# The down product of a gated MLP as seven-product blocks with a transposed output

## The chip, the core and the metric

The kernel runs on one core of a Trainium2 chip. Its engines are TensorE (PE, matrix products; PEld is its weight load), VectorE (DVE), ScalarE (ACT), GpSimd (POOL) and SyncE (SP), which mostly starts transfers. The metric is the device time of a run in microseconds; the kernel before takes 717.9 us (median of 3 runs, 716.68 to 718.46).

## The reference

Rotary attention over 4 x 8 heads of 576 positions of 64, then a gated MLP over the 2304 tokens:

```python
x = attention(rotate(q), rotate(k), v)          # 2304 x 512
g = x @ w_gate                                  # 512 x 1536
silu = g * (1.0 / (1.0 + np.exp(-g)))
val = x @ w_val
out = (silu * val) @ w_out                      # 1536 x 512
```

## The kernel before

Every matrix product of the MLP is made in three passes of a 32-bit reduced format: an operand is split into a high half (a copy that rounds) and a low half (operand minus high), and hi x hi, hi x lo and lo x hi are accumulated in PSUM. The split is written `split` (line 678): the copy on ScalarE, the subtract on VectorE or GpSimd.

Attention fills the first 280 us. Then `plain` multiplies the first 256 columns of w_gate and w_val directly, while the weights of the rest are prepared. From some 336 us, `strassen` makes the other 1280 columns in ten weight steps s: pair fp = 1 + s // 2, and i = s % 2 says gate (0) or value (1). A weight step has three units, one for each third p of the tokens in the order 1, 2, 0 (`ORDER`); a third is two blocks of 384 tokens. A unit is one 2 x 2 block product in seven products (`PROD`) of six matmuls of 384 columns (line 824), each product in a PSUM bank of its own, of a ring of six. VectorE, ScalarE and GpSimd put the seven together (lines 808, 827). One unit later `finish` (line 846) applies silu where i is 0, and `keep` stores gate or value to two DRAM buffers, hf for the first 7 tiles of 128 tokens, ht for the other 11.

Beside it runs a stream of jobs (`Stream`), each one raw 512 KB block of weights: a load, a ScalarE instruction and six VectorE instructions that turn stored bits into numbers (lines 734 to 741). 20 jobs are w_gate and w_val, 12 are w_out; `strassen` takes two or three of them in a weight step.

The down product follows in `finish` (line 1341), in two stages. In the first, for each of 12 blocks f of 128 hidden rows: HF is loaded from hf (line 876), VectorE multiplies gate by value (line 882), the product and a w_out block are split, lows on GpSimd, and seven PSUM banks accumulate 3 matmuls of 512 columns each (line 892). In the second, each of 11 token tiles is loaded from ht, multiplied and split on VectorE (line 928) and gets 36 matmuls of 512 columns (line 941). Results are token rows; ScalarE copies them out of PSUM (line 901) and SP stores them.

From the last part of attention to the end, the order of instructions is the written one on all of PE, ACT, DVE, SP and POOL (`manual_schedule`); elsewhere a planner orders them by program order and the readiness that it expects. SP's queue is in written order, and a transfer at its head waits there until its buffer is free.

Of the kernel before, what the change touches and what calls it, by code (L numbers as in the profile page):

```python
# [19 lines left out]
NT = B * S  # L20
# [477 lines left out]
FT, NX = 7, 3  # L498
PROD = [(0, "B", 0), (5, "T", 3), (4, "T", 0), (6, "T", 1), (2, "T", 2), (1, "B", 1), (7, "B", 2)]


class Moe:
    def __init__(self, tc, keep, pl, yd, rd, hd, wg, wv, wo, out):
        self.tc, self.nc = tc, tc.nc
        self.yd, self.rd, self.hd, self.w, self.wo, self.out = yd, rd, hd, (wg, wv), wo, out
# [25 lines left out]
    def xbuf(self, pool, blk):  # L531
        p, b = divmod(blk, 2)
        if b == 0:
            self.xa[p] = [self.own(pool, f"xa{p}{x}", [128, 4, BK]) for x in "hl"]
        else:
            self.xm[p] = [self.own(pool, f"xm{p}{x}", [128, 2, BK]) for x in "hl"]
            self.xb[p] = [self.own(pool, f"xb{p}{x}", [128, 2, BK]) for x in "hl"]

    def wform(self, pool, i):
        self.W[i] = [self.own(pool, f"W{i}{x}", [128, 8, 256]) for x in "hl"]  # L540
# [20 lines left out]
    def open_late(self, ctx):  # L561
# [7 lines left out]
        self.WF = [self.own(one, f"WF{i}", [128, 8, 256], FP32) for i in range(2)]  # L569
# [6 lines left out]
    def open_mid(self, ctx):  # L576
# [4 lines left out]
        self.own(one, "HF1", [128, FT, 2, 128], FP32)  # L581
# [198 lines left out]
    def ev(self, u, ps):  # L780
# [9 lines left out]
        sv = sv.rearrange("p (t i q) -> p t i q", i=2, q=128)  # L790
        nc.scalar.activation(out=sv[:, :, 0], in_=ps[0].rearrange("p (t q) -> p t q", q=128), func=ACTF.Silu)
        nc.scalar.copy(sv[:, :, 1], ps[1].rearrange("p (t q) -> p t q", q=128))
        self.keep(f, 9 * s + 3 * t, sv.rearrange("p t i q -> p t (i q)"), slice(0, 2), nc.sync if u else nc.scalar)

    def keep(self, f, t, x, i, q):
        n = x.shape[1]
        m = min(max(FT - t, 0), n)
        if m:
            q.dma_start(out=self.hd[0][f, :, t:t + m, i].rearrange("p t i q -> p t (i q)"), in_=x[:, 0:m])
        if m < n:  # L800
            t = t + m - FT
            q.dma_start(out=self.hd[1][t:t + n - m, :, f, i].rearrange("t p i q -> p t (i q)"), in_=x[:, m:n])

    def unit(self, fp, i, p):
# [3 lines left out]
        add = lambda e, out, in0, in1: e.tensor_tensor(out=out, in0=in0, in1=in1, op=ALU.add)  # L808
        sg = [self.again(f"xm{p}{x}", [128, 2, BK], FP32, "sg") for x in "hl"]
        dst = [sg[k // 2][:, k % 2] for k in range(4)]  # L810
        (ah, al), (bh, bl), (Th, Tl) = self.xa[p], self.xb[p], self.T[p]
        B = [(ah[:, 0:2], al[:, 0:2]), (ah[:, 2:4], al[:, 2:4]), (bh, bl)]
        c1, u, z5 = (self.c_p.tile([128, BK], FP32, name=n) for n in ("c1", "u", "z5"))
        for k, (w, kind, x) in enumerate(PROD):
            acc = self.ch()[:, 0:BK]
# [5 lines left out]
            for c in range(2):  # L821
                rh, rl = xh[:, c], xl[c] if isinstance(xl, list) else xl[:, c]
                for l, r in ((Wh, rh), (Wh, rl), (Wl, rh)):
                    nc.tensor.matmul(acc, l[:, w, c * 128:(c + 1) * 128], r, start=(n == 0), stop=(n == 5))  # L824
                    n += 1
            if k in (0, 2):
                ac.copy((c1, None, z5)[k], acc)  # L827
            if k == 2 and self.after:
                self.after.pop(0)()
# [15 lines left out]
    def finish(self, fp, i, p, sg):
        for j in range(2):
            if i == 0:
                self.nc.scalar.activation(out=sg[j], in_=sg[j], func=ACTF.Silu)
            self.keep(2 * fp + j, 6 * p, sg[j].rearrange("p j (t q) -> p (j t) q", q=128), slice(i, i + 1), self.nc.sync)

    def osplit(self, f):
        g, k = divmod(f, 4)
        if k == 0:
            self.Ot = [self.again(f"{('W0', 'T1', 'T2')[g]}{x}", [128, 4, DM], F32R, f"O{x}") for x in "hl"]
        Oh, Ol = self.O[f] = [t[:, k] for t in self.Ot]
        return self.split(self.nc.gpsimd, Oh, Ol, self.of(f))
# [534 lines left out]
```

## Time and profile before

| | |
|---|---|
| Median of the runs | 717.9 us |
| The profiled execution | span 715.3 us |
| Busy: PE, DVE, POOL, ACT | 694.9, 539.7, 476.8, 409.1 us |
| Ten weight steps | 336.4 to 558.6 us |
| First down stage (L892) | 558.6 to 619.5 us |
| Second down stage (L941) | 619.5 to 711.3 us |

Busy times are sums over an engine's instructions. A group of instructions is named by line, engine, operation and tile (out<-in), with partitions x elements. The chain of waits is followed back from the last instruction: what stands in it was waited for. A wait names the engine that waits, its line, and what released it.

### The profile page before, as it was taken

What the parts mean: (1) busy time and instruction counts of PE and PEld (TensorE: products, weight loads), DVE (VectorE), ACT (ScalarE), POOL (GpSimd) and SP (SyncE); (2) the same over time, 40 slices, a digit from 0 to 9 for tenths busy, and PEclk for the clock granted to TensorE, in tenths of its full rate; (3) what the DMA queues carried; (4) which work ended last, traced back from release to release, by engine and by line L of the source; (5) the groups of instructions that cost most, each with busy time, mean ns of one, the idle gap of its engine ahead of it and who ended that gap; (6) DMA issues with size and microseconds to landing.
All of it is one profiled execution on the core that took longest, in us unless ns stands there. A gap on an engine that the chain in (4) does not pass through costs nothing.

```text
span 715.3 us, 12744 instructions
## 1 busy us (share of the span) xinstructions
PE 694.9 (97%) x4342; PEld 654.6 (92%) x4342; DVE 539.7 (75%) x884; ACT 409.1 (57%) x892; POOL 476.8 (67%) x473
## 2 busy tenths in 40 slices
PE   8999999999999999999799999999999999999997
PEld 7899999999999999988799999999999877888887
DVE  5888898888888887848898868778677893455451
ACT  5899998888888887357443524334243332433331
POOL 8899799999999966659976576655675767200000
PEclk9999999999999999999999999999999999999999
DMA  6887899779887895973465565646648865786671
GB/s 189 208 224 203 218 226 258 197 200 259 226 215 195 203 264 169 222 227 111 125 188 165 167 182 155 192 148 182 180 118 277 282 227 178 307 282 220 206 221 30
DMA packets 111329, 143.86 MB, mean 201 GB/s; under 512 B 17808, under 2 KB 86048, under 8 KB 111264
## 3 DMA queue, kind: packets, MB, share of 16 engines
q1 hardware_dynamic: 110240, 141.97, 69.9%
q10 hardware_dynamic: 1024, 1.07, 0.5%
q8 instruction: 35, 0.57, 0.3%
q14 instruction: 30, 0.25, 0.1%
HBM read 76.35 MB, written 42.54 MB: 166 GB/s over the span
## 4 chain that ended last, share of the span: by engine, by line
PE 77%; DVE 9%; ACT 6%; DMA 4%; POOL 1%; issue 1%; SPq 0%; DVEq 0%; ACTq 0%; POOLq 0%
PE ch L824 28%; PE ch L941 13%; PE pv L459 11%; PE sc L343 10%; PE tr L419 8%; DMA HF<-hf 3%; PE ch L892 2%; PE tr L283 2%; ACT E L376 1%; ACT N L302 1%; DVE HF L882 1%; PE ch L776 1%; POOL fl L678 1%; DVE raw L738 1%; DVE T2l L678 1%
## 5 line engine op out<-in xcount | busy, mean ns | idle before, releaser
L358 DVE TENSOR_REDUCE nmt<-sc 128x1 f32<-128x576 f32 x144 | 108.3, 752 | 20.2 <-PE sc L343 18.7
L376 ACT ACTIVATE E<-sc,nmt 128x576 f32<-128x576 f32 x128 | 97.5, 762 | 1.2 <-DVE nmt L358 1.1
L808 POOL TENSOR_TENSOR u<-u,z 128x384 f32<-128x384 f32 x30 | 30.5, 1015 | 71.3 <-DVE sg L808 69.2
L419 PE MATMUL tr<-ident,E 128*128 128x128 f32 x512 | 77.0, 273 | 0.4 <-DVE ET1l L421 0.2
L419 PEld LDWEIGHTS tr<-ident,E 128*128 128x128 f32 x512 | 61.1, 141 | 3.3 <-PE tr L283 1.4
L827 ACT COPY c<-ch 128x384 f32<-128x384 f32 x30 | 14.4, 481 | 81.6 <-PE ch L824 47.5
L200 POOL TENSOR_TENSOR t<-X,tab 128x256 f32<-128x256 f32 (+2 forms) x94 | 54.1, 597 | 10.2 <-DMA X<-in_qk_dram 6.4
L343 PE MATMUL sc<-QK 128*128 128x288 f32 x240 | 58.6, 325 | 1.3 <-ACT E L376 0.4
L420 ACT CAST ET2h<-tr 128x512 fp32r<-128x512 f32 x80 | 47.2, 590 | 15.9 <-PE tr L419 15.6
L421 DVE TENSOR_TENSOR ET2l<-tr,ET2h 128x512 fp32r<-128x512 f32 x80 | 53.2, 683 | 2.2 <-ACT ET2h L420 2.0
L678 DVE TENSOR_TENSOR hl<-hg,hh 128x384 fp32r<-128x384 f32 x44 | 25.8, 587 | 37.7 <-ACT hh L678 37.7
L941 PE MATMUL ch<-Oh,hh 128*128 128x512 f32 (+1 forms) x144 | 54.0, 375 | 0.0
L941 PE MATMUL ch<-Ol,hh 128*128 128x512 f32 (+1 forms) x144 | 53.8, 374 | 0.0
L941 PE MATMUL ch<-Oh,hl 128*128 128x512 f32 (+1 forms) x144 | 53.8, 374 | 0.0
L343 PE MATMUL sc<-N,QZ 128*128 128x288 f32 x240 | 51.4, 296 | 0.0
L202 POOL TENSOR_TENSOR rot<-rot,t 128x512 f32<-128x512 f32 (+2 forms) x47 | 47.0, 1000 | 3.7
L421 DVE TENSOR_TENSOR ET1l<-tr,ET1h 128x512 fp32r<-128x512 f32 x64 | 43.1, 686 | 6.9 <-ACT ET1h L420 6.4
L201 POOL TENSOR_TENSOR rot<-X,tab 128x512 f32<-128x512 f32 (+2 forms) x47 | 47.1, 1002 | 0.0
L678 ACT CAST hh<-hg 128x384 fp32r<-128x384 f32 x44 | 22.6, 514 | 41.5 <-DVE hg L928 41.5
L808 DVE TENSOR_TENSOR sg<-ch,u 128x384 f32<-128x384 f32 x60 | 33.4, 556 | 16.5 <-PE ch L824 13.0
L420 ACT CAST ET1h<-tr 128x512 fp32r<-128x512 f32 x64 | 36.9, 597 | 13.0 <-PE tr L419 13.0
L459 PE MATMUL pv<-ET2h,VS 128*128 128x320 f32 x128 | 40.7, 328 | 1.0 <-ACT ET2h L420 0.9
(413 smaller groups left out, 2414.7 us busy)
## 6 DMA issues: line engine op xcount, KB each, us to landing
QK<-N SPq DMA_DIRECT2D x64, 288.0 KB, 4.2
hg<-ht SPq DMA_DIRECT2D x22, 768.0 KB, 7.1
HF<-hf SPq DMA_DIRECT2D x12, 896.0 KB, 5.1
X<-in_qk_dram SPq DMA_DIRECT2D x15, 576.0 KB, 5.0
yd<-Y SPq DMA_DIRECT2D x31, 256.0 KB, 4.6
ht<-sg SPq DMA_DIRECT2D x20, 384.0 KB, 3.6
hf<-sg SPq DMA_DIRECT2D x20, 384.0 KB, 3.7
ht<-sg SPq DMA_DIRECT2D x20, 320.0 KB, 3.1
```

The lines of the kernel that those rows point to most:

```text
L200: e.tensor_tensor(out=sel(t2, u), in0=sel(x, w), in1=tb(Sn, u), op=ALU.mult)
L343: nc.tensor.matmul(ps[:, g, 0:288], l, rr[:, o + g * 288:o + (g + 1) * 288], start=(x == 0), stop=(x == len(terms) - 1))
L358: nc.vector.tensor_reduce(out=nmcol, in_=ps[:, :, 0:288], axis=AX.XY, op=ALU.max, negate=True)
L376: nc.scalar.activation(out=E.rearrange("p (a b) -> p a b", a=2), in_=ps[:, :, 0:288], func=ACTF.Exp, bias=nmcol, scale=1.0, accum_out=self ...
L419: nc.tensor.transpose(ps[:, c], E[:, o + c * 128:o + (c + 1) * 128], self.ident)
L420: nc.scalar.copy(dst[0], src)
L421: nc.vector.tensor_tensor(out=dst[1], in0=src, in1=r32(dst[0]), op=ALU.subtract)
L459: nc.tensor.matmul(st["ps"][:, 0:w], VS[:, sl, :], t, start=(x == 0), stop=(x == last))
L678: return [lambda: self.nc.scalar.copy(h, f), lambda: le.tensor_tensor(out=l, in0=f, in1=r32(h), op=ALU.subtract)]
L808: add = lambda e, out, in0, in1: e.tensor_tensor(out=out, in0=in0, in1=in1, op=ALU.add)
L824: nc.tensor.matmul(acc, l[:, w, c * 128:(c + 1) * 128], r, start=(n == 0), stop=(n == 5))
L941: self.nc.tensor.matmul(ps, l[:, f], r[:, z], start=(n == 0), stop=(n == 3 * NFF - 1))
```

## The change

The down product is made in the same seven-product scheme. A round n is a third of the tokens; in each of its seven steps k, TensorE takes a 2 x 2 block form of w_out (weights, in 128 x 128 pieces) and a form of the gated product (384 moving columns), 36 matmuls in two halves j. The result comes out transposed, hidden rows first, and the host reorders it.

- In the up product, the order of the seven products is changed, and the last three accumulate in PSUM onto banks of earlier ones (`ONTO`). The value unit multiplies by the gate at once; gate and value stay on chip, and only their product is stored, once a pair and third, for the first pair gate and value as before.
- w_out's forms are made in the job stream (`obits`: four GpSimd sums for the second half of a block), stored to DRAM from ACT's queue and loaded again in `Down.oload`.
- `strassen` takes 2 to 4 jobs in a weight step (`TAKE`), 29 in all, and none in the last.
- `Down` loads blocks B11, B21, B12, B22 of the product for each round, makes the sums and the splits of the next step during a step (`form`, `osplit`), and starts in the last weight step (`lead`). For round 0 the last piece of each block comes from the chip (`late`).
- From `strassen` on, only SP and PE keep the written order.

```diff
...
-FT, NX = 7, 3
-PROD = [(0, "B", 0), (5, "T", 3), (4, "T", 0), (6, "T", 1), (2, "T", 2), (1, "B", 1), (7, "B", 2)]
+NFP = NFF // 2
+PROD = [(0, "B", 0), (5, "T", 3), (4, "T", 0), (6, "T", 1), (1, "B", 1), (7, "B", 2), (2, "T", 2)]
+ONTO = {4: 0, 5: 2, 6: 3}
...
     def unit(self, fp, i, p):
         nc = self.nc
         ve, po, ac = nc.vector, nc.gpsimd, nc.scalar
...
+        tt = lambda e, out, in0, in1, op=ALU.add: e.tensor_tensor(out=out, in0=in0, in1=in1, op=op)
+        if i == 0:
+            g = self.G[p] = self.again(f"xm{p}", [128, 4, BK], FP32, "sg")
+            dst = [g[:, k] for k in range(4)]
+        else:
+            if self.V is None:
+                self.V = self.r_p.tile([128, 4, BK], FP32, name="R")
+            g, v = self.G[p], self.V
+            dst = [g[:, 0]] + [v[:, k] for k in range(1, 4)]
...
+        accs = []
         for k, (w, kind, x) in enumerate(PROD):
-            acc = self.ch()[:, 0:BK]
+            accs.append(accs[ONTO[k]] if k in ONTO else self.ch()[:, 0:BK])
+            acc = accs[k]
...
+            if k == 0:
+                ac.copy(u, acc)
+            elif k == 1:
+                tt(ve, u, acc, u)
+                if self.after:
+                    self.after.pop(0)()
+            elif k == 2:
+                ac.copy(z5, acc)
             elif k == 3:
+                tt(ve, dst[3], acc, u)
+                tt(po, dst[3], dst[3], z5)
+                if i:
+                    tt(po, g[:, 3], v[:, 3], g[:, 3], ALU.mult)
+            elif k == 4 and i == 0:
+                ac.activation(out=dst[0], in_=acc, func=ACTF.Silu)
             elif k == 4:
+                tt(ve, dst[0], acc, dst[0], ALU.mult)
             elif k == 5:
+                tt(ve, dst[1], acc, u)
+            else:
+                tt(ve, dst[2], acc, u)
+                self.after.append(lambda: self.finish(fp, i, p, g, v if i else None))
             yield k
 
...
+    def finish(self, fp, i, p, g, v):
+        nc = self.nc
+        if i == 0:
+            nc.scalar.activation(out=g[:, 1:4], in_=g[:, 1:4], func=ACTF.Silu)
+            return
+        nc.gpsimd.tensor_tensor(out=g[:, 1:3], in0=v[:, 1:3], in1=g[:, 1:3], op=ALU.mult)
+        if (fp, p) != (NFP - 1, ORDER[0]):
+            (nc.sync if fp < NFP - 1 else nc.scalar).dma_start(out=self.hd[p][fp - 1], in_=g)
...
+
+    def obits(self, half, fp):
+        nc, F = self.nc, self.FO
+        tt = nc.gpsimd.tensor_tensor
...
+
+        def end():
+            last()
+            if half == 0:
+                nc.scalar.dma_start(out=self.od[0][fp], in_=F[:, 0:2])
+                return
+            nc.scalar.dma_start(out=self.od[1][fp], in_=F[:, 3])
+            for o, a, b, op in ((4, 2, 3, ALU.add), (6, 0, 2, ALU.subtract), (5, 4, 0, ALU.subtract),
+                                (7, 1, 5, ALU.subtract)):
+                tt(out=F[:, o], in0=F[:, a], in1=F[:, b], op=op)
+            nc.scalar.dma_start(out=self.od[2][fp], in_=F[:, 4:8])
+        return ops + [end]
...
-    strassen(moe, J, S, Z)
-    finish(moe, S)
+    strassen(moe, J, S, Z).run()
...
+    o = [(h, fp) for fp in range(NFP) for h in range(2)]
     for s in range(10):
-        for h in range(2):
-            job("w", s, h)
-        if s in (4, 6, 8):
-            job("o", 2 + s // 2)
-    for f in (0, 1, 2, 3, 7, 8, 9, 10, 11):
-        job("o", f)
+        job("w", s, 0)
+        if s >= 4:
+            job("o", *o.pop(0))
+        job("w", s, 1)
+        if s in (5, 8):
+            job("o", *o.pop(0))
+    for x in o:
+        job("o", *x)
...
+TAKE = (2, 3, 3, 4, 3, 3, 4, 3, 4)
...
+    dn = Down(moe)
+    for q, k, f in dn.lead():
+        at(9, q, k, f)
...
-        dq = S.take(n, s < 9)
+        dq = S.take(TAKE[s], s < 8) if s < 9 else []
...
+SUMS = {2: ("TT", "B12", "B11"), 3: ("TT", "B22", "TT"), 4: ("B12", "B22", "B12"), 6: ("TT", "B21", "TT")}
+FORM = ("B11", "B21", "TT", "TT", "B12", "B22", "TT")
+OFORM = ((0, 0), (0, 1), (2, 0), (2, 1), (2, 2), (2, 3), (1, 0))
+LOAD = {2: ("B11",), 5: ("B21", "B12"), 6: ("B22",)}
+MULT = {4: ("B11",), 6: ("B21", "B12")}
+RAW = {"B11": ("T1h", 0), "B21": ("T1l", 2), "B12": ("T2h", 1), "B22": ("T2l", 3)}
+
+
+class Down:
+
+    def lead(self):
+        ve = self.nc.vector
+        return [
+            (0, 0, self.first), (0, 1, lambda: self.oload(0, slice(0, 5))), (0, 5, lambda: self.osplit(0, ve, slice(0, 5))),
+            (1, 0, lambda: self.vload(0, "xb1")), (1, 0, lambda: self.load(0, "B11")),
+            (1, 0, lambda: self.load(0, "B21")), (1, 4, lambda: self.late("B11")), (1, 4, lambda: self.late("B21")),
+            (1, 4, lambda: self.oload(0, slice(5, 6))), (1, 4, lambda: self.oload(1)),
+            (2, 0, lambda: self.load(0, "B12")), (2, 0, lambda: self.load(0, "B22")), (2, 0, lambda: self.late("B12")),
+            (2, 0, lambda: self.late("B22")), (2, 0, lambda: self.mult(0, "B11", ve)),
+            (2, 1, lambda: self.osplit(0, ve, slice(5, 6))),
+            (2, 1, lambda: self.form(0, ve)), (2, 4, lambda: self.mult(0, "B21", ve)), (2, 5, lambda: self.osplit(1, ve)),
+        ]
...
+    def oload(self, k, z=slice(0, NFP)):
...
+        h, x = OFORM[k]
+        self.nc.sync.dma_start(out=r32(self.O[k][1])[:, z], in_=self.moe.od[h][z, :, x].rearrange("f p d -> p f d"))
+
+    def osplit(self, k, e, z=slice(0, NFP)):
+        Oh, Ol = (x[:, z] for x in self.O[k])
+        self.nc.scalar.copy(Oh, r32(Ol))
+        e.tensor_tensor(out=Ol, in0=r32(Ol), in1=r32(Oh), op=ALU.subtract)
+
+    def vload(self, n, slot=None):
+        m, p = self.moe, ORDER[n]
+        for x in range(2):
...
+            self.nc.sync.dma_start(out=v, in_=m.hv[p][:, 2 * x:2 * x + 2, 1])
+            self.V[x] = v
+
+    def load(self, n, b):
+        m, p = self.moe, ORDER[n]
+        slot, k = RAW[b]
+        r = self.raw[b] = m.again(slot, [128, NFP, BK], FP32, "d" + b)
+        self.nc.sync.dma_start(out=r[:, 0], in_=m.hv[p][:, k, 0])
+        f = NFP - 2 if n == 0 else NFP - 1
+        self.nc.sync.dma_start(out=r[:, 1:1 + f], in_=m.hd[p][0:f, :, k].rearrange("f p q -> p f q"))
+
+    def late(self, b):
+        self.nc.sync.dma_start(out=self.raw[b][:, NFP - 1], in_=self.moe.G[ORDER[0]][:, RAW[b][1]])
+
+    def mult(self, n, b, e):
+        r, k = self.raw[b][:, 0], RAW[b][1]
+        e.tensor_tensor(out=r, in0=r, in1=self.V[k // 2][:, k % 2], op=ALU.mult)
+
+    def form(self, s, e, se=None):
+        k = s % 7
+        if k in SUMS:
+            o, a, b = SUMS[k]
+            se.tensor_tensor(out=self.raw[o], in0=self.raw[a], in1=self.raw[b], op=ALU.subtract)
+        src = self.raw[FORM[k]]
+        hi, lo = self.H[s % 2]
+        for z in (slice(0, 3), slice(3, NFP)):
+            self.nc.scalar.copy(hi[:, z], src[:, z])
+            e.tensor_tensor(out=lo[:, z], in0=src[:, z], in1=r32(hi)[:, z], op=ALU.subtract)
...
+    def run(self):
+        nc, m = self.nc, self.moe
+        ve, po, ac = nc.vector, nc.gpsimd, nc.scalar
+        self.open()
+        self.oload(2)
+        self.oload(3)
+        self.oload(4)
+        self.mult(0, "B12", ve)
+        self.mult(0, "B22", ve)
+        for s in range(N):
+            n, k = divmod(s, 7)
+            if n and k == 0:
+                self.mult(n, "B22", po)
+            if s + 1 < N:
+                n1, k1 = divmod(s + 1, 7)
+                if n == 0 and 0 < k < 6:
+                    self.osplit(k + 1, po)
+                self.form(s + 1, ve, ve if n1 == 0 or k1 == 3 else po)
+            if n == 0 and k < 2:
+                self.oload(k + 5)
+            if n < 2 and k == 2:
+                self.vload(n + 1)
+            for b in LOAD.get(k, ()) if n < 2 else ():
+                self.load(n + 1, b)
+            for b in MULT.get(k, ()) if n < 2 else ():
+                self.mult(n + 1, b, po)
+            for j in range(2):
...
+                if k == 0:
+                    ac.copy(t["u"], ps)
+                elif k == 1:
+                    ac.copy(t["o11"], ps)
+                    self.out(n, "o11", j)
+                elif k == 2:
+                    ac.copy(t["z"], ps)
+                elif k == 3:
+                    add(ve, t["u"], ps, t["u"])
+                elif k == 4:
+                    add(ve, t["o22"], ps, t["u"])
+                    add(po, t["o22"], t["o22"], t["z"])
+                    self.out(n, "o22", j)
+                elif k == 5:
+                    add(ve, t["o12"], ps, t["u"])
+                    self.out(n, "o12", j)
+                else:
+                    add(ve, t["o21"], ps, t["u"])
+                    self.out(n, "o21", j)
```

## Rows read from the trace of the kernel before

**Rows 1.** The page, part 1: busy us, share of the span, instructions.
```profile
span 715.3 us, 12744 instructions
...
PE 694.9 (97%) x4342; PEld 654.6 (92%) x4342; DVE 539.7 (75%) x884; ACT 409.1 (57%) x892; POOL 476.8 (67%) x473
```
**Rows 2.** The chain that ended last, in order of time: start, length, what.
```profile
355.71 200.98 PE ch L824 x1157
...
619.58 91.75 PE ch L941 x432
...
711.36 0.37 ACT o L901
```
**Rows 3.** Stages: length, busy us (instructions) of each engine, TensorE's clock, DMA share, GB/s.
```profile
core 0: us, PE busy (x) PEld busy (x) DVE busy (x) ACT busy (x) POOL busy (x), PEclk, DMA share, GB/s
300.00:320.00 20.00, 19.72 (x113) 19.08 (x111) 10.75 (x19) 8.64 (x19) 13.33 (x13) 1.00 0.91 249
336.40:358.00 21.60, 17.91 (x100) 17.01 (x100) 19.80 (x27) 10.49 (x17) 21.21 (x16) 1.00 0.41 121
...
490.00:512.00 22.00, 22.00 (x129) 22.00 (x128) 15.66 (x29) 8.94 (x15) 13.55 (x12) 1.00 0.65 191
535.00:558.40 23.40, 23.40 (x137) 23.40 (x136) 17.75 (x31) 7.23 (x14) 13.03 (x11) 1.00 0.91 284
```
**Rows 4.** TensorE's waits from 558.4 to 619.4 us: total, times, longest.
```profile
PE ch L892 <- POOL fl L678: 2.4, 4, 1.0
```
**Rows 5.** Timeline from 602 to 608 us: start, length, instruction, [idle before <-releaser].
```profile
603.29 2.11 POOL L678 TENSOR_TENSOR fl<-HF,fh 128x896 fp32r<-128x896 f32 x1 [2.84 <-ACT fh L678]
...
603.97 2.38 DVE L882 TENSOR_TENSOR HF<-HF 128x896 f32<-128x896 f32 x1 [1.78 <-DMA HF<-hf]
...
605.37 2.14 POOL L678 TENSOR_TENSOR Ol<-OF,Oh 128x512 fp32r<-128x512 f32 x1
...
605.46 0.50 PE L892 MATMUL ch<-Oh,fl 128*128 128x512 f32 x1 [0.56 <-POOL fl L678]
```
**Rows 6.** GpSimd's groups after 384 us: busy us, mean ns, idle before.
```profile
L678 POOL TENSOR_TENSOR fl<-HF,fh 128x896 fp32r<-128x896 f32 x12 | 25.5, 2125 | 17.0 <-ACT fh L678 17.0
...
L678 POOL TENSOR_TENSOR Ol<-R,Oh 128x512 fp32r<-128x512 f32 x3 | 3.9, 1299 | 0.0
```
**Rows 7.** Timeline from 327 to 362 us: GpSimd, VectorE, then ScalarE.
```profile
333.13 7.43 POOL L684 TENSOR_TENSOR R<-R 128x768 f32<-128x768 f32 x3
340.52 1.85 POOL L684 TENSOR_TENSOR Z<-xa0h,xa0l 128x768 f32<-128x768 f32 x1
342.32 1.02 POOL L684 TENSOR_TENSOR Z<-xm0h,xm0l 128x384 f32<-128x384 f32 x1
...
333.79 5.89 DVE L678 TENSOR_TENSOR T2l<-T0h,T2h 128x1536 fp32r<-128x1536 f32 x2
...
353.90 1.76 DVE L678 TENSOR_TENSOR T0l<-R,T0h 128x1536 fp32r<-128x1536 f32 x1
...
352.40 1.47 ACT L678 CAST T0h<-R 128x1536 fp32r<-128x1536 f32 x1
```
**Rows 8.** Timeline from 414 to 419 us, GpSimd and VectorE.
```profile
415.69 2.42 POOL L678 TENSOR_TENSOR W0l<-WF,W0h 128x1024 fp32r<-128x1024 f32 x1
...
417.25 0.56 DVE L808 TENSOR_TENSOR sg<-ch,u 128x384 f32<-128x384 f32 x1 [0.86 <-PE ch L824]
```
**Rows 9.** Line 892: min/median/max ns, first and last start.
```profile
L892 PE MATMUL ch<-Oh,fh x84: 389/389/402, 558.6 to 618.7; 128*128 128x512 f32 x84
```
**Rows 10.** Tile HF: min/median/max ns, first and last start.
```profile
L882 DVE TENSOR_TENSOR HF<-HF x12: 1091/1152/2382, 549.9 to 610.0; 128x896 f32<-128x896 f32 x12
```
**Rows 11.** DMA issues: queue, count, KB each, median us to landing.
```profile
HF<-hf SPq DMA_DIRECT2D x12, 896.0 KB, 5.1
...
out_dram<-o SPq DMA_DIRECT2D x2, 128.0 KB, 3.2
out_dram<-o SPq DMA_DIRECT2D x4, 64.0 KB, 2.2
```
**Rows 12.** VectorE's groups from 384 to 556.8 us: busy us, mean ns, idle before.
```profile
L808 DVE TENSOR_TENSOR sg<-ch,u 128x384 f32<-128x384 f32 x48 | 26.8, 557 | 14.9 <-PE ch L824 13.0 <-POOL WF L961 0.3
...
L737 DVE TENSOR_SCALAR aux<-aux 128x512 uint32<-128x512 uint32 x19 | 13.1, 692 | 0.2
```

More of the change, by code (lines that the diff above doesn't have):

```diff
@@ L568, in open_late @@
         self.wform(one, 0)
-        self.WF = [self.own(one, f"WF{i}", [128, 8, 256], FP32) for i in range(2)]
+        w = self.own(one, "WF", [128, 2, 8, 256], FP32)
+        self.WF = [w[:, x] for x in range(2)]
         self.Z = [self.own(one, f"T0l{c}", [128, 4, BK], FP32) for c in range(2)]
@@ L580, in open_mid @@
         self.wform(one, 1)
-        self.own(one, "HF1", [128, FT, 2, 128], FP32)
+        self.FO = self.own(one, "FO", [128, 8, 256], FP32)
         self.c_p = pool("m_cp", 2)
@@ L823, in unit @@
                 for l, r in ((Wh, rh), (Wh, rl), (Wl, rh)):
-                    nc.tensor.matmul(acc, l[:, w, c * 128:(c + 1) * 128], r, start=(n == 0), stop=(n == 5))
+                    nc.tensor.matmul(acc, l[:, w, c * 128:(c + 1) * 128], r, start=(n == 0 and k not in ONTO),
+                                     stop=(n == 5), skip_group_check=True)
                     n += 1
[L826 to L829, printed above, removed]
@@ L843, in unit @@
             yield k
[L845 to L856, printed above, removed]
@@ L884, in fdown @@
-    def fdown(self, f):
-        hh, hl = self.fs.pop(f)
-        Oh, Ol = self.O[f]
-        for t in range(FT):
-            if f == 0:
-                self.ps[t] = self.ch()
-            sl = slice(128 * t, 128 * t + 128)
-            for n, (l, r) in enumerate(((hh, Oh), (hh, Ol), (hl, Oh))):
-                self.nc.tensor.matmul(self.ps[t], l[:, sl], r, start=(f == 0 and n == 0), stop=(f == NFF - 1 and n == 2))
-            if f == NFF - 1:
-                self.give(t, slice(0, DM), self.ps[t])
@@ L896, in give @@
-    def give(self, t, z, ps):
-        nc = self.nc
-        if z.start == 0:
-            self.ot = self.again(f"xm{t % 2}{'hl'[t // 2 % 2]}", [128, DM], FP32, "o")
-        o = self.ot
-        nc.scalar.copy(o[:, z], ps)
-        s, k = divmod(t, 9)
-        if k < 8:
-            b, i = divmod(k, 4)
-            r0 = (2 * s + b) * S
-            nc.sync.dma_start(out=self.out[r0:r0 + 512, z].rearrange("(p r) d -> p r d", r=4)[:, i], in_=o[:, z])
-        else:
-            for g in range(2):
-                r0 = (2 * s + g) * S + 512
-                nc.sync.dma_start(out=self.out[r0:r0 + 64, z], in_=o[64 * g:64 * g + 64, z])
@@ L1332, in strassen @@
                 g += 1
-                t = g if s else min(g, 7) + max(0, g - 14)
+                t = min(g, 7) + max(0, g - 14) if s == 0 else g
                 run(dq, t * m // (21 if s else 14) - (m - len(dq)))
-    run(moe.after)
-    assert not own
-    for f in range(2, 4):
-        run(moe.osplit(f))
-def finish(moe, S):
-    for f in range(NFF):
-        if S.begun < len(S.jobs):
-            S.sign()
-        if f + 2 < NFF:
-            run(moe.fsplit(f + 2))
-        else:
-            moe.hload(FT + f - NFF + 2)
-        if f + 1 == NFF:
-            run(moe.hsplit(FT))
-        if f + 3 < NFF:
-            moe.fload(f + 3)
-        if S.ops:
-            run(S.take(1, False))
-        if f + 4 < NFF:
-            run(moe.osplit(f + 4))
-        moe.fdown(f)
-    for t in range(FT, 18):
-        if t + 2 < 18:
-            moe.hload(t + 2)
-        if t + 1 < 18:
-            run(moe.hsplit(t + 1))
-        moe.down(t, 1 + (t == 17))
+    while moe.after:
+        moe.after.pop(0)()
```

195 lines of the change are left out of this document (95 added, 100 removed).

## The prediction, before the run

> **What bounds the kernel now.** I read the busy table first: TensorE is busy for 694.9 of 715.3 us, the next engine for three quarters of them [rows 1]. Then the chain of waits, in order of time: from 355.71 us it is one block of 1157 matmuls of 384 columns, and at the end one of the down product's, 91.75 us without a break [rows 2]. So from 356 us on, whatever takes matmul columns away is worth its full time, unless operands come late. A matmul of 384 columns costs 200.98 / 1157 = 0.1737 us there; the granted clock is 1.00, the 2.4 GHz level, in every stretch read [rows 2, 3]. The only operands that come late in the old down product are low halves that GpSimd makes: TensorE waited 2.4 us for them, in four waits [rows 4].
>
> What stands behind that wait is the place to look at longest. At 603.29 GpSimd subtracts for 2.11 us, both operands in SBUF. VectorE starts a multiply of two SBUF operands at 603.97 and needs 2.38 us; it ends 0.95 us after GpSimd does. GpSimd's next subtract, 1.30 us elsewhere, takes 2.14, and the matmul at 605.46 comes late [rows 5, 6]. Earlier the same: two VectorE subtracts of 1536 take 5.89 us, where one takes 1.76, and the three GpSimd subtracts beside them 7.43, where alone they take 1.85 + 1.02 + 1.02 = 3.89. As 3.89 + 2 x 1.76 = 7.41, they ran strictly in turn [rows 7]. A VectorE add with one operand in PSUM is not touched: 0.56 us inside a GpSimd subtract that keeps its 2.42 us [rows 8]. I call it the shared turn.
>
> The Trainium skill, SBUF — State Buffer, section Who interferes with whom, has this as a rule: a VectorE instruction with two SBUF inputs and a GpSimd instruction that reads SBUF exclude each other, and the one that starts second is blocked until the first has ended. By that rule the two engines' times of such work are added, which speaks against this change; the sum below goes by the rows, which agree.
>
> **What the change does, priced.** *Matmuls.* The old down product runs from 558.6 [rows 9] to 619.58 + 91.75 = 711.33 [rows 2]: 152.7 us. The new one has 3 rounds x 7 steps x 2 halves x 6 blocks x 3 products = 756 matmuls of 384 columns: 756 x 0.1737 = 131.3 us, 6.25 us a step. Gain: 21.4 us if TensorE never waits. The up product keeps its 1260 matmuls, 42 a unit (7.3 us).
>
> The Trainium skill, TensorE: Matmul & The Clock Gate, section Back-to-back issue gap, gives N/2.4 + 2.5 ns for a warm stream. By it such a matmul takes 162.5 ns and the new product 122.9 us, 8.4 less; the rows have 173.7 in just this kind of stream, so I use the rows.
>
> *Operands of the down product.* All its sums, high copies and low subtracts go from SBUF to SBUF. VectorE takes 1.09 us for 896 elements [rows 10] and 1.76 for 1536 [rows 7], 1.05 ns an element: 0.56 for 384, 1.36 for 1152, 2.56 for 2304. GpSimd takes 1.30 for 512 and 2.13 for 896 [rows 6], 2.15 ns: 3.5 for 1536, 5.15 for 2304. The form of a step is two low subtracts, 2.72.
>
> Round 0. What must pass the shared turn between the moment when the last weight step frees its first unit's buffers (two units, 14.6 us, before the down product) and the start of step 6 (6 x 6.25 = 37.5 us into it), 52.1 us in all: seven forms 19.0; four sums on VectorE 10.2; five splits of w_out on GpSimd 17.5; the splits of blocks 0 and 1 on VectorE 3.7; four multiplies 2.2; GpSimd's three multiplies of 768 that finish the last units 5.5, and four short ones 4.1; two adds and a multiply in step 4, 3.0. That is 65.2 us, so step 6 comes at least 13.1 us late even if the turn is never idle. It is idle at the start: from the same moment to the w_out block of step 2 (O2), the queues must move the values of the first units 0.4 MB, two blocks 2.0, their last pieces 0.4, w_out 0.9, two more blocks 2.0 and pieces 0.4, one or two stores of 0.8 and O2 itself 0.8: 7.6 to 8.4 MB. They moved 249 GB/s at a busy share of 0.91 and 284 at 0.91, so 274 to 312 at most [rows 3]: 24 to 31 us, and some 2 us to land (64 KB take 2.2) [rows 11]. O2 is there 12 to 18 us into the down product; with 1.47 for its copy [rows 7] and 3.5 for its split, step 2, due at 12.5, starts 4 to 10 us late. From the copy on, 34 us of turn work remain (five splits, four forms, a sum, step 4's three), so step 6 starts 47 to 53 us in, 10 to 16 late: the same answer. With lows that may be written only after the step that frees their buffer, I take 16 for round 0; bounds 4 (the turn binds nothing, only the transfers) and 22.
>
> Round 1: seven forms 19.0, three GpSimd sums 15.5, a VectorE sum 2.6, four multiplies 4.1, two adds 2.0: 43.2 of 43.8 us. Round 2 up to its step 6: six forms 16.3, the same sums 18.1, a multiply and two adds 3.1: 37.5 of 37.5. In the old stretch from 558.6 to 619.6 the turn held 12 x 2.13 + 10 x 1.30 + 12 x 1.09 = 52 of 61 us [rows 6, 10], and TensorE lost 2.4 (4%) [rows 4]. At 99% it loses more: a VectorE instruction can stand 5.15 us behind one GpSimd sum, and behind it in VectorE's queue stand the adds that empty PSUM. Bounds 0 and 16 over 81 us; I take 8.
>
> *Up product.* Products 1, 7 and 2 accumulate onto banks that were read before. That saves VectorE an add a unit where i is 0, and GpSimd one of two adds. It adds a wait: the fifth to seventh product wait until ACT or VectorE has read the bank, filled two or three products (2.1 us or more) earlier; behind such a matmul stands all of TensorE's queue. The add is 0.56 us and one instruction of the weight stream before it 0.69 [rows 12], 1.25 together, so hidden by 0.8 us; 0.5 to 1 us a unit if VectorE lags. It may: weight steps 1 to 8 take 27 jobs of the stream, not 20, of six VectorE instructions of 0.69, + 29.0 us against 12 x 0.56 = 6.7 saved. VectorE was busy for 15.7 of 22 us [rows 3]; + 22.3 over 8 steps of 21.9 us makes 84%. The finishing multiplies go to GpSimd: 13.6 of 22 becomes some 19 where i is 1 [rows 3]. Eighteen stores of w_out's forms and two of the product stand in ACT's queue and wait there for GpSimd; behind them stand the copies of u and z, for which TensorE's fifth and sixth product wait. The order on the three engines is no longer the written one, which can gain or lose. Bounds -2 (of the 3.7 us lost at 336 to 358 [rows 3] half is won back) and +8; I take +2: VectorE fills, but does not overflow.
>
> *At nothing:* the stores of gate and value that become 14 of the product, the loads of hf and ht that become 12 blocks, and w_out's eight reloads: all on queues under matmuls; where that cover goes, at the start, they are in O2's lateness above. The transposed output costs no instruction here. *Tail:* the last add is 0.56 [rows 12], the copy was 0.37 [rows 2]; 192 KB leave in place of 128 (128 KB take 3.2 us, 896 KB 5.1) [rows 11]: + 0.3 in all.
>
> **Sum.** 715.3 - 21.4 + 16 + 8 + 2 + 0.3 = 720.2 us of span. The median of the runs, 717.9, lies 2.6 above this execution's span: 722.8, say 723.
>
> **Rivals.**
> *The shared turn hides.* If splits and sums fall into gaps and work done ahead covers rounds 1 and 2, only the transfers at the start cost: 715.3 - 21.4 + 7 + 0 to 4 + 1.3 + 2.6 = 705 to 709. For it: 16 of the 21 steps need no w_out split, and adds from PSUM run beside GpSimd freely [rows 8]. Against: round 0 is over-full by count, not by order. It decides if less than 52 us of round 0's work excludes each other. This is the case on the faster side.
> *The start runs dry.* Blocks come in pieces of 1 and 1.5 KB over one in-order queue, in which last pieces wait for GpSimd and two blocks for the second unit; and an engine whose order puts the multiply of an unlanded block first stalls with it. With O2 at 18 us, round 0 at + 22 and the later rounds at + 12: 733. For it: 300 to 320 us, where pieces of 1.5 KB are loaded, is the stretch with 274 GB/s for a full share [rows 3]. Against: 896 KB land in 5.1 us [rows 11].
> *VectorE overflows in the up product.* If its share passes some 95%, the short reach of the bank reuse costs 0.3 us in each of 24 units, + 7 in place of 2: 728.
> That no columns are saved is excluded by count: 648 x 512 against 756 x 384.
>
> **How the numbers follow.** Forecast (719 to 728) 0.45; turn hidden (700 to 716) 0.27; start dry (729 to 738) 0.18; VectorE overflows 0.10. A difference under 0.3% (715.7 to 720.1) is what a measurement here cannot tell from none. Faster: nearly all of the second case, 0.25. Same: the rest of it, the low edge of the forecast, and the last case where rounds 1 and 2 cost little, 0.12. Slower: what is left, 0.63. The range 706 to 736 leaves out the best of the second case and the worst of the third; the forecast's own is 719 to 728.
>
> **What would show it.** Right: the down product's block of the chain broken in round 0, TensorE released by VectorE and GpSimd at steps 2 to 6; GpSimd's splits of 1536 at 3.5 us alone and 5 to 6 beside VectorE; steps of 8 to 10 us in round 0 and nearer 6.25 later; O2 landing 12 us or more after the first down matmul. Wrong: 756 matmuls in under 140 us, or VectorE's subtracts of 1152 at 1.36 us with GpSimd busy beside them. More than 203 us from 356 us to the first down matmul would move the cause to the up product.

## The result, and the profile after

The changed kernel takes 725.9 us (median; 725.75 to 728.06) beside 717.3 for the kernel before on the same chip (716.26 to 718.46): ratio 1.013, 95% interval 1.0108 to 1.0151. Slower by 1.3%, though the down product streams an eighth fewer columns through TensorE (756 x 384 in place of 648 x 512).

The profiled execution has a span of 724.0 us, 8.7 more than before. I cut it at the first matmul of the up product, at the first of the down product, there at every 36th matmul (one step), and at the end of the last one, all from the timeline.

| Stretch, us | before | after | difference | forecast |
|---|---|---|---|---|
| start to first up matmul | 335.5 | 336.4 | + 0.9 | 0 |
| up product | 223.1 | 227.3 | + 4.2 | + 2 |
| down product | 152.7 | 156.8 | + 4.1 | + 2.6 (- 21.4 + 16 + 8) |
| tail | 4.0 | 3.5 | - 0.5 | + 0.3 |

The matmuls of one round of the new down product were counted at 43.8 us. Its three rounds took 57.8, 50.5 and 48.5: 14.0, 6.7 and 4.7 over the count.

The page, as in [rows 1]: TensorE is less busy in a longer span, and VectorE goes from 75% to 82%.

```profile
span 724.0 us, 12703 instructions
...
PE 687.5 (95%) x4414; PEld 668.3 (92%) x4414; DVE 593.7 (82%) x848; ACT 426.0 (59%) x873; POOL 541.0 (75%) x498
```

TensorE's waits in the down product (563 to 721 us: total, times, longest), where [rows 4] had 2.4 us in all:

```profile
PE ch L1437 <- DVE dWF L1378: 9.2, 4, 3.3
...
PE ch L1437 <- DVE dW L1378: 2.6, 3, 1.0
...
PE ch L1437 <- ACT du L1442: 2.0, 1, 2.0
```

So TensorE waits mostly for low halves of the product's forms (line 1378), which VectorE makes. With two short waits of 0.9 and 0.5 all waits come to 15.2 us. Of the rest of the 25.4 us over the count, some 7 are matmuls that no wait holds up and that stand 0.32 us apart in place of 0.174 (3.0, 2.2 and 1.9 us in the three rounds): TensorE's clock was at half behind the longer waits, as the last section says. Why the lows are late is in the timeline of round 0, steps 1 to 3 (GpSimd, then VectorE, then TensorE's waits):

```profile
576.70 3.46 POOL L1345 TENSOR_TENSOR dO<-dO 128x1536 fp32r<-128x1536 f32 x1 [8.74 <-ACT dO L1344]
...
580.55 4.15 POOL L1345 TENSOR_TENSOR dO<-dO 128x1536 fp32r<-128x1536 f32 x1 [0.39 <-ACT dO L1344]
...
584.66 4.57 POOL L1345 TENSOR_TENSOR dO<-dO,dW 128x1536 fp32r<-128x1536 f32 x1
```
```profile
577.72 8.21 DVE L1378 TENSOR_TENSOR dWF<-dT,dW 128x1152 fp32r<-128x1152 f32 x2 [1.34 <-ACT dW L1377]
585.96 5.70 DVE L1373 TENSOR_TENSOR dT<-dB,dT 128x2304 f32<-128x2304 f32 x1
592.92 2.63 DVE L1378 TENSOR_TENSOR dW<-dT,dH 128x1152 fp32r<-128x1152 f32 x2 [1.27 <-ACT dH L1377]
```
```profile
581.43 0.45 PE L1437 MATMUL ch<-dWF,dO 128*128 128x384 f32 x1 [3.25 <-DVE dWF L1378]
585.97 0.69 PE L1437 MATMUL ch<-dWF,dO 128*128 128x384 f32 x1 [2.38 <-DVE dWF L1378]
```

The two lows that take 2.63 us at 592.92, with GpSimd idle, took 8.21 beside two of GpSimd's splits; the sum took 5.70 where it takes 2.55 alone. It is a strict alternation, as in [rows 7]: the first split ends at 580.16, the first low 1.3 later (TensorE starts on it at 581.43); the second split 3.3 after that, at 584.70; the second low 1.2 later (585.97); the third split at 589.23, the sum at 591.66. The chain's last break, in round 2, is the same: a GpSimd sum, then a low of 1152 that takes 6.18 us in place of 1.35, behind GpSimd's next sum, and then TensorE (GpSimd's next sum, then the chain):

```profile
681.01 5.13 POOL L1373 TENSOR_TENSOR dB<-dB,dB 128x2304 f32<-128x2304 f32 x1
```
```profile
673.68 6.30 POOL dT L1373
...
680.00 1.17 ACT dW L1377
...
681.19 6.18 DVE dWF L1378
...
687.41 33.09 PE ch L1437 x179
...
720.52 0.56 DVE do L1440
```

The longest break of round 1 has another last step. GpSimd's sum takes 5.93 us, ScalarE's cast waits 6.25 us for it, u's copy stands behind that cast, and TensorE, whose second product goes on in u's bank, waits 2.04 for the copy (GpSimd, ScalarE, TensorE):

```profile
625.64 5.93 POOL L1373 TENSOR_TENSOR dT<-dB,dB 128x2304 f32<-128x2304 f32 x1 [2.04 <-DMA out_dram<-do]
```
```profile
631.60 1.15 ACT L1377 CAST dH<-dT 128x1152 fp32r<-128x1152 f32 x1 [6.25 <-POOL dT L1373]
632.66 0.47 ACT L1442 COPY du<-ch 128x384 f32<-128x384 f32 x1
```
```profile
633.19 0.44 PE L1437 MATMUL ch<-dW,dO 128*128 128x384 f32 x1 [2.04 <-ACT du L1442]
```

The low behind GpSimd's next sum then costs 0.65 more, at 638.98. So here most of the wait comes from a long sum on GpSimd (5.11 us for 2304 at 632.60, where VectorE takes 2.56) by way of ScalarE, and not from a low that stands behind it.

The stages, columns as in [rows 3] (the last two are new stretches, of rounds 0 and 2):

```profile
336.40:358.00 21.60, 17.98 (x92) 17.02 (x91) 19.03 (x25) 12.03 (x19) 21.13 (x15) 0.92 0.27 85
490.00:512.00 22.00, 21.26 (x123) 20.95 (x122) 20.15 (x36) 9.27 (x14) 15.08 (x14) 1.00 0.41 136
535.00:558.40 23.40, 23.40 (x137) 23.40 (x136) 17.25 (x28) 8.30 (x12) 10.98 (x10) 1.00 0.54 182
582.00:595.00 13.00, 9.14 (x39) 8.05 (x38) 11.69 (x4) 3.97 (x6) 7.23 (x2) 0.74 0.52 182
686.00:699.00 13.00, 11.59 (x57) 11.59 (x58) 11.34 (x7) 5.51 (x7) 3.70 (x2) 0.87 0.04 15
```

In the up product 336 to 358 has 8 matmuls fewer than before (1.4 us), and 490 to 512, full before, 6 fewer (1.0); VectorE was busy for 20.2 of those 22 us, before for 15.7.

### The profile page after: what moved, and what is told of

It reads as the page before. It is cut to its first block, busy times and chain, and to the rows that moved or that the text cites. A ratio compares the mean times of both kernels' runs of the same rounds, so it can differ in the third digit from the quotient of the medians.

```text
span 724.0 us, 12703 instructions
## 1 busy us (share of the span) xinstructions
PE 687.5 (95%) x4414; PEld 668.3 (92%) x4414; DVE 593.7 (82%) x848; ACT 426.0 (59%) x873; POOL 541.0 (75%) x498
## 5 line engine op out<-in xcount | busy, mean ns | idle before, releaser
L364 DVE TENSOR_REDUCE nmt<-sc 128x1 f32<-128x576 f32 x144 | 108.2, 751 | 20.2 <-PE sc L349 18.9
L1437 PE MATMUL ch<-dW,dO 128*128 128x384 f32 x252 | 78.4, 354 | 3.7 <-ACT du L1442 2.0
L691 POOL TENSOR_TENSOR W<-WF,W 128x1024 fp32r<-128x1024 f32 x20 | 47.9, 2408 | 11.5 <-ACT W L691 11.5
L1437 PEld LDWEIGHTS ch<-dW,dO 128*128 128x128 f32 x252 | 49.9, 202 | 5.0 <-ACT du L1442 2.4
L1437 PE MATMUL ch<-dH,dO 128*128 128x384 f32 x180 | 50.6, 339 | 1.4 <-DVE dO L1345 0.9
L837 PE MATMUL ch<-T0h,W 128*128 128x384 f32 x160 | 44.1, 337 | 1.1 <-DVE sg L813 0.5
L837 PE MATMUL ch<-T2h,W 128*128 128x384 f32 x160 | 44.0, 336 | 0.6 <-DVE sg L813 0.6
L837 PE MATMUL ch<-T1h,W 128*128 128x384 f32 x160 | 43.9, 335 | 0.0
L841 ACT COPY u<-ch 128x384 f32<-128x384 f32 x30 | 14.3, 477 | 45.6 <-PE ch L837 40.8
```

The source lines that it names most:

```text
L364: nc.vector.tensor_reduce(out=nmcol, in_=ps[:, :, 0:288], axis=AX.XY, op=ALU.max, negate=True)
L691: return [lambda: self.nc.scalar.copy(h, f), lambda: le.tensor_tensor(out=l, in0=f, in1=r32(h), op=ALU.subtract)]
L1437: nc.tensor.matmul(ps, l[:, f, d], r[:, f], start=(a == k and f == 0 and x == 0), stop=(f == NFP - 1 and x == 2), skip_group_check=True)
```

## The experiments

Theory: the shared turn (VectorE and GpSimd both working from SBUF to SBUF) is what the down product loses. Rivals: the transfers at its start; the scheduler's order; and for the up product, the reuse of PSUM banks. All twelve runs, in us (stretches from each run's profiled execution, cut as above; up: first up matmul to first down matmul):

| Run | median | ratio to before (95%) | up | round 0 | round 1 | round 2 |
|---|---|---|---|---|---|---|
| changed kernel | 725.9 | 1.0108 to 1.0151 | 227.3 | 57.8 | 50.5 | 48.5 |
| e1 sums on VectorE | 717.9 | 0.9979 to 1.0007 | 227.5 | 57.4 | 46.2 | 44.2 |
| e2 splits on VectorE | 719.9 | 1.0008 to 1.0036 | 227.9 | 53.5 | 47.7 | 48.5 |
| e3 all on VectorE | 713.2 | 0.9899 to 0.9949 | 228.4 | 54.8 | 44.2 | 44.2 |
| e4 block loaded early | 729.0 | 1.0127 to 1.0169 | 228.6 | 60.7 | 48.7 | 48.7 |
| e5 e3 + reading adds | 783.4 | 1.0870 to 1.0932 | 229.3 | 65.2 | 55.1 | 53.2 |
| e6 e3 + fills | 711.4 | 0.9870 to 0.9930 | 227.8 | 54.6 | 44.2 | 44.2 |
| e7 e3, written order, up too | 733.9 | 1.0187 to 1.0239 | 256.2 | 48.3 | 44.2 | 44.3 |
| e8 ScalarE written in up | 756.6 | 1.0501 to 1.0555 | 256.3 | 60.8 | 48.5 | 48.0 |
| e9 e3, written order in down | 707.2 | 0.9837 to 0.9886 | 227.8 | 49.8 | 44.2 | 44.3 |
| e10 cast pinned | 729.8 | 1.0130 to 1.0184 | 233.7 | 57.4 | 50.2 | 48.5 |
| e11 e9 + e10 | 710.6 | 0.9884 to 0.9924 | 230.4 | 49.9 | 44.5 | 44.3 |
| e12 written order in down alone | 724.4 | 1.0080 to 1.0122 | 227.7 | 60.1 | 48.9 | 48.2 |

**e1 and e2: one part of GpSimd's work moved.**

```
e1: - self.form(s + 1, ve, ve if n1 == 0 or k1 == 3 else po)
    + self.form(s + 1, ve, ve)
e2: - self.osplit(k + 1, po)
    + self.osplit(k + 1, ve)
```

> Only the six sums of 2304 of rounds 1 and 2 go from GpSimd to VectorE. Theory (the shared turn costs the later rounds their 11.2 us): a sum takes 2.6 us of the turn in place of 5.1, the turn of round 1 falls from 43.2 to 35.5 us of 43.8, so rounds 1 and 2 lose 3 to 5 us in place of 11.2: about 719, and the pairs of lows that took 7.4 to 7.6 us take 2.7. Rival (what is late is an engine's order or the transfer of a block, not the turn): 725 to 727. Rival (VectorE is full): slower than 727.

> Only the five splits of w_out of 1536 in round 0 go from GpSimd to VectorE. Theory (the shared turn): each takes 1.76 us of the turn in place of 3.5, 8.7 us less in all, so round 0 falls from 58.0 to 50 to 53 us: 718 to 721. Rival (round 0 waits for the transfers of the w_out blocks): a split that waits for its transfer now stands ahead of the lows in VectorE's queue; 724 to 730.

Both times are as the theory has it. e1 takes 8.0 us off: rounds 1 and 2 took 90.4 us in place of 99.0, and round 0 hardly changes. A sum on VectorE is also half as long, so e1 does not tell the length of GpSimd's sums from the turn; e5 and e6 do that for the turn. One wait of 1.57 us is left in round 1, behind a block that landed late: VectorE's sum at 624.99 had waited 5.93 us for it. e2 takes 6.0 off: 4.3 in round 0, which is less than the 8.7 us by which the turn gets shorter, and 2.8 in round 1, which has no split; why round 1 gained is not shown.

**e3: all of it moved.** Both edits, and `po` becomes `ve` in the multiplies and in the add for o22.

> Nothing of the down product is left on GpSimd: sums, splits, multiplies and adds all on VectorE. Theory (the shared turn): VectorE has 47 us of work in 44 us of round 0 and some 36 of 44 in the others, and nothing to wait its turn for: lows of 1152 at 1.36 us throughout, round 0 at 48 to 51 us, rounds 1 and 2 at 44 to 46 each: 708 to 713, below the kernel before. Rival (VectorE becomes the bound, its queue stands behind transfers): 718 to 726.

713.2: faster than the kernel before. Rounds 1 and 2 have no wait (44.2 us each, lows at 1.35), and TensorE runs unbroken from step 3 of round 0:

```profile
591.00 116.19 PE ch L1437 x647
```

Round 0 took 54.8, more than the 48 to 51 expected. VectorE had no idle time from 580 to 590 us and worked in an unhelpful order: splits of steps 4 and 5 (line 1345) ahead of the lows of step 3, for which TensorE waited at 591.00.

```profile
584.99 1.76 DVE L1345 TENSOR_TENSOR dO<-dO,dW 128x1536 fp32r<-128x1536 f32 x1
586.65 1.36 DVE L1378 TENSOR_TENSOR dWF<-dB,dW 128x1152 fp32r<-128x1152 f32 x1
587.92 1.76 DVE L1345 TENSOR_TENSOR dO<-dO,R 128x1536 fp32r<-128x1536 f32 x1
589.59 2.63 DVE L1378 TENSOR_TENSOR dW<-dT,dH 128x1152 fp32r<-128x1152 f32 x2
```

**e4: the transfer rival.** `self.oload(2)` moves from `run` to ahead of the loads of B12 and B22 in `lead`.

> Only the load of the w_out block of step 2 is issued earlier, ahead of two blocks of the product. Theory (the shared turn, over-full by count in round 0): step 2 starts earlier but step 6 does not; 724 to 726. Rival (the start runs dry, round 0 waits for that block's landing): round 0 loses 4 to 6 us less: 719 to 722.

It took 3 us more than the changed kernel. The two intervals overlap, so a loss is not shown; but it is no gain, which the rival had forecast. The block came earlier, so GpSimd split it at 569.23 in place of 576.70. A VectorE multiply of 384, 0.55 us alone, met that split, and TensorE waited 3.10 us, at 574.83, for a copy behind it:

```profile
569.23 4.56 POOL L1345 TENSOR_TENSOR dO<-dO 128x1536 fp32r<-128x1536 f32 x1
```
```profile
570.41 3.80 DVE L1367 TENSOR_TENSOR dB<-dB,dV 128x384 f32<-128x384 f32 x1
```

An earlier landing of this block does not shorten round 0. The theory's time (724 to 726) was missed as well: it left out that an earlier landing brings an earlier collision. The edit also puts two blocks of the product later in the queue, so it does not clear the transfers as a whole. e3 and e9 say more of them: with the queue of the changed kernel, round 0 falls to 54.8 and 49.8 us. With the turn gone a transfer is in the way again: the chain that ended last in e9 runs through the landing of a w_out block at 574.71.

```profile
560.46 14.25 DMA dO<-od
```

**e5 and e6: the turn by itself.** To e3, whose down product has nothing on GpSimd, 126 GpSimd instructions are added whose results nobody uses, on two tiles of their own:

```
+ for _ in range(6):                                         # each of 21 steps
+     po.tensor_tensor(out=dx, in0=dx, in1=dy, op=ALU.add)   # e5
+     po.memset(dx, 0.0)                                     # e6
```

> The kernel with the down product all on VectorE (713.2 us), and beside it on GpSimd 126 adds of 384 elements with both operands in SBUF, on two tiles that nothing else uses; some 1.0 us each, so GpSimd is busy for about the whole of the down product. Theory (work from SBUF to SBUF on the two engines goes in turn): each of VectorE's 24 to 29 such instructions of a round waits for an add under way, 0.5 to 1 us, and its 37 to 47 us of a round become 52 to 70 of 44: 733 to 755, lows of 1152 at 2 us or more in place of 1.36. Rival (the later rounds lost their time to the length of GpSimd's sums or to the order, not to the turn): 712 to 716, lows at 1.36.

> The same 126 places, but each a fill of the 384 elements with a constant, which reads nothing. Theory (it is the reading of SBUF by both that excludes, not GpSimd being busy or writing): lows of 1152 stay at 1.36 us; 711 to 715. Rival (any GpSimd instruction beside VectorE costs): 718 or more, in between by the length of the fills.

e6: no cost (711.4 beside e3's 713.2). But the fills bunch: all 126, of 0.42 us each, stand between 560.4 and 625 us, beside round 0 and the start of round 1. So round 0 is where the two runs compare: 54.6 us with the fills, 65.2 with the reading adds, 54.8 with neither. e5: the down product took 173.6 us where e3's took 143.1. Its total missed the expectation (733 to 755), since the adds, themselves held up, took 204 us in place of some 126 and went on for 43 us after the last matmul; the down product itself ended at 739.0. In e6 (GpSimd first, then VectorE) a low takes 1.36 us inside a row of 67 fills without a gap; in e5 it takes 2.16 inside a row of adds, which take 2.16 each in place of 0.99:

```profile
580.06 31.88 POOL L1416 MEMSET u<- 128x384 f32 x67
```
```profile
585.59 1.36 DVE L1378 TENSOR_TENSOR dWF<-dB,dW 128x1152 fp32r<-128x1152 f32 x1
```
```profile
637.97 25.95 POOL L1416 TENSOR_TENSOR u<-u,z 128x384 f32<-128x384 f32 x12
```
```profile
643.59 2.16 DVE L1378 TENSOR_TENSOR dW<-dT,dH 128x1152 fp32r<-128x1152 f32 x1
```

Apart from their length (0.42 and 0.99 us), what the added instructions of the two kernels differ in is whether GpSimd reads SBUF. This is the rule of the Trainium skill, SBUF — State Buffer, section Who interferes with whom, down to its exception for an instruction that only writes; both runs agree with it.

**e12: the order alone.** `with tc.manual_schedule(engines={Activation, DVE})` around `dn.run()`; GpSimd keeps its work.

> The changed kernel with VectorE and ScalarE in the written order in the down product, and GpSimd left with its splits, sums and multiplies. Theory (the shared turn is what costs): the down product keeps most of its 25.7 us over the bare matmuls, 16 to 26: 716 to 726. Rival (the scheduler's order, not the turn, made the loss): the down product at 137 to 143 us as with all on VectorE, 706 to 713.

The down product took 157.2 us, beside 156.8 in the changed kernel. In the written order too, two lows take 8.19 us beside GpSimd's splits:

```profile
575.96 8.19 DVE L1380 TENSOR_TENSOR dWF<-dT,dW 128x1152 fp32r<-128x1152 f32 x2 [4.06 <-ACT dW L1379]
```

So the scheduler's order alone is not the cause of the loss. It matters once the turn is gone: e7 and e9.

**e8 and e10: the up product.** e8 holds ScalarE to the written order around `strassen(...)`. e10 pins one instruction: `moe.tc.keep_in_program_order(...)` around the cast that makes T0's high half.

> The changed kernel (725.9 us) with one thing undone: in the up product ScalarE's instructions stand in the written order, so the copy of the first unit's u is ahead of the cast that waits for GpSimd's sums. Theory (the up product's + 4.0 us is that one wait of 3.0 and the half clock behind it): no wait at 340 us, no half clock there, 721 to 724. Rival (the reuse of banks costs in every unit, VectorE lags): 725 to 727, waits of the same sum elsewhere.

> The changed kernel (725.9 us) with one instruction pinned: the cast of T0's high half stays behind the second unit's copy of u, instead of ahead of the first unit's. Theory (the up product's + 4.0 us is that wait of 3.0 us and the half clock behind it): 721 to 723, first down matmul 3 to 4.5 us earlier. Rival (the bank reuse waits as long elsewhere): 725 to 727.

Both missed; my reading of the up product's + 4.2 fell. In the changed kernel the first unit's fifth product waits 2.99 us for the copy of u, which stands behind a cast that waits for GpSimd (ScalarE's cast and copy, then TensorE):

```profile
341.49 1.47 ACT L691 CAST T0h<-R 128x1536 fp32r<-128x1536 f32 x1 [2.92 <-POOL R L697]
...
343.23 0.48 ACT L841 COPY u<-ch 128x384 f32<-128x384 f32 x1
```
```profile
343.77 0.65 PE L837 MATMUL ch<-xa1h,W 128*128 128x384 f32 x1 [2.99 <-ACT u L841]
```

In e10 that copy is done at 338.3, and TensorE waits 4.07 us two products later, for a bank that VectorE has to read first (GpSimd, VectorE, TensorE), and 2.3 us for T0's low half, whose high half is what the pinned cast makes:

```profile
333.04 7.41 POOL L697 TENSOR_TENSOR R<-R 128x768 f32<-128x768 f32 x3
```
```profile
333.70 5.89 DVE L691 TENSOR_TENSOR T2l<-T0h,T2h 128x1536 fp32r<-128x1536 f32 x2
...
343.69 0.55 DVE L813 TENSOR_TENSOR u<-ch,u 128x384 f32<-128x384 f32 x1
```
```profile
345.95 0.45 PE L837 MATMUL ch<-T1h,W 128*128 128x384 f32 x1 [4.07 <-DVE sg L813]
```

VectorE is behind because its lows ran in turn with GpSimd's sums, as before the change [rows 7], and stream work (339.51 to 343.78 us) stands in its queue ahead of the add. Behind either engine the reused bank makes TensorE wait. e8 shows the other fear of the prediction: in the written order ScalarE's stores of w_out wait for GpSimd, and u's copy behind them. TensorE waited 16.3 us for it, and ScalarE 19.7 for line 894:

```profile
ACT u L841 <- POOL FO L894: 19.7, 2, 12.9
...
PE ch L837 <- ACT u L841: 16.3, 6, 6.3
```

The scheduler's order on ScalarE is worth about 29 us here (256.3 against 227.3).

**e7, e9 and e11: what beats both.** e7 and e9 are e3 with VectorE and ScalarE in the written order in the down product, the sum put ahead of the split in each step of round 0; e7 keeps ScalarE to it in the up product as well. e11 is e9 with e10's pin.

> All of the down product on VectorE, its instructions and ScalarE's there in the written order (sum, split, lows of the next step, step by step) in place of the scheduler's, and ScalarE in the written order in the up product too. In the run before, VectorE was full in round 0 and made three w_out splits (1.76 us each) ahead of lows that were due sooner. Theory (round 0 is now VectorE's own time and its order, 47 us of work in 44): steps 1 to 3 lose 5 to 8 us in place of 10.9, and the first up unit 3 less: 703 to 709. Rival (a written order has no work done ahead, and every step of round 0 is late by what VectorE has over 6.25 us): 712 to 718.

> All of the down product on VectorE and in the written order on VectorE and ScalarE there; the up product as in the changed kernel. In the run that had ScalarE in the written order in the up product too, the new down product took 136.6 us, 6.4 less than with the scheduler's order, and the up product 26 more. Theory (the two parts are independent, and what is left of round 0 is the order of VectorE's own work): 713.2 - 6.4 = 706 to 708. Rival (the down product was only that short because the late up product had given its loads and lows a head start): 711 to 714.

> Both: all of the down product on VectorE in the written order, and the cast pinned. If both effects add: 702 to 705; if the pin brings nothing: 706 to 708.

e7 lost in the up product what e8 lost; its down product, 136.8 us, is 5.5 over the count of its matmuls. e9 keeps the up product and gets 707.2, 1.4% under the kernel before (0.9837 to 0.9886). Its down product took 138.4, so of the 6.3 us that e7's had saved against e3's, 4.7 came from the order. The other 1.6 I put down to the head start that e7's late up product gave; no run shows it by itself. From step 6 of round 0 TensorE runs unbroken:

```profile
607.20 94.72 PE ch L1442 x539
```

The pin costs 3.4 us in e11 (against e9); e10's median is 3.9 over the changed kernel's, though there the intervals overlap.

## Why the prediction was right, point by point

- **The matmuls' gain, - 21.4: right, 1.2 too large.** 756 matmuls; a step without a wait took 6.24 to 6.44 us (forecast 6.25), and a round without one 44.2 (counted 43.8). The sizes below are over the count, so they hold this.
- **Round 0, + 16: right in cause and nearly in size (14.0).** The count said 65.2 us of turn work between the last weight step's freed buffers and step 6. From there to step 6 it took 14.6 + 51.6 = 66.2. That the two are so near is in part luck: in these 66.2 us the turn was in use for 60.1, taking both engines' work from SBUF to SBUF together, and idle for 6. e2 and e3 show that shortening the turn shortens the round. The side argument on transfers was mis-sized: they moved 382 GB/s from 560 to 575 us where I had allowed 312, and the w_out block was there 11.4 us in, not 12 to 18.
- **Rounds 1 and 2, + 8: right in direction, too small (11.4), and the cause is only in part the one forecast.** The low that stands behind a GpSimd sum was forecast; it makes the break in step 2 of round 2 (10.29 us) and short waits elsewhere. The break in step 1 of round 1 (10.13) comes mainly from a sum's length, through ScalarE and a reused bank, for which the forecast had no term. Nor had it one for the clock: of the 11.4 us, waits are 5.9 and slow matmuls 4.1. The turn was not full either: it was in use for 42.7 of the 50.5 us of round 1, so the count alone does not give the loss. e1 shows that GpSimd's sums are behind most of it (8.6 us).
- **Up product, + 2: too small, 4.2.** I had half of the old loss at 336 to 358 won back; none was. The wait of 2.99 for the copy of u, at a reused bank, is new, and four shorter ones of 0.5 to 0.7 follow. VectorE did fill (84% forecast, 92% measured from 490 to 512), and only short waits came of it. The named waits add up to 5.3 us against 3.7 before; slow matmuls at half clock, most of them behind the first wait, cost 2.3 against 0.2, and 0.4 us stays unexplained. How to be rid of the first wait stays open: e8 and e10 moved it.
- **Tail: + 0.3 forecast, - 0.5 measured.** No step hangs on it. Nor on the + 0.9 ahead of the up product: over the profiles of all kernels here it starts between 333.7 and 337.6 us.
- **Rivals.** "The turn hides" is out by e1 to e3. "The start runs dry" had the block of step 2 landing at 18 us, and it was there at 11.4; e4 gained nothing by an earlier one. "VectorE overflows" gave part of the up product's loss and none of the down product's: with all its work on VectorE alone (e9) the down product is 18 us shorter.
- **Signs.** As forecast, TensorE waits for low halves in round 0, and splits and lows are slower beside each other. But no wait of TensorE there ended with GpSimd, GpSimd's splits took 4.15 to 4.77 us where 5 to 6 was forecast, and one step took 15.2 us in place of several at 8 to 10. One sign against the forecast did show: from 356 us to the first down matmul it took 207.7 us, over the 203 named. By the stretches, 5.1 of the 8.7 us lie ahead of the down product, whose own 25.4 us over the count are mostly set off by the matmuls' gain.

The errors were of one sign in three terms (+ 3.4 in rounds 1 and 2, + 2.2 up, + 0.9 ahead of it) and of the other in round 0 (- 2.0) and the tail (- 0.8), so they cancelled in part, which is luck: the span came out 3.8 over the forecast. The median lay 1.9 above the profiled span, not 2.6, so the time is 3.1 over 722.8, inside its own range.

## What to carry to other kernels

Count the work of VectorE with two SBUF operands and of GpSimd reading SBUF as one engine's work, stage by stage: where the sum nears the matmul time, moving work to GpSimd costs its full, longer duration, and moving it back to VectorE gained 12.7 us here with VectorE at 100% in places. Adds with an operand in PSUM (0.55 us throughout), casts on ScalarE (1.16 us for 1152, at 633.03 beside a sum and a low) and fills on GpSimd (e6) don't count in it. A sum under the matmul time does not clear a stage: look also at one long instruction and at what stands behind it, and allow for slow matmuls behind the longer waits. Where an accumulation goes on in a bank that another engine must read first, ask what else stands in that engine's queue, since TensorE's whole queue waits behind it.

## What the runs showed of the hardware

- TensorE's granted clock fell to its 1.2 GHz level after short idle times: behind the wait of 2.99 us at 343.77 the matmuls of the changed kernel stand 0.32 us apart in place of 0.174, until 347.1; likewise in 582 to 595 (0.74) and 686 to 699 (0.87). Before, no stretch read was under 1.00 [rows 3]. In the up product it is not a cost that I could show: e9 had the same wait (2.98) at a clock of 1.00 from 336 to 358, and its up product took 227.8 us against 227.3, with a wait of 0.81 in the slow matmuls' place. In round 2 it is one: no wait follows the one at 687.41, and of the 179 matmuls behind it those from 688.6 to 692.0 (clock 0.50) make the round 1.9 us longer.
- With both queues full, as in e5 from 638 to 664 us, the two engines alternate one instruction each: 2.16 us for a low that takes 1.36 and 2.16 for an add that takes 0.99.
